# Fused attention and SwiGLU on one core: earlier V loads, AV products behind scores, and FFN partial sums ahead of the last pair

## The chip, the core and the metric

The kernel runs on one core of a Trainium2 chip. A core has five engines that work side by side, each through its own queue in order: TensorE (PE, matrix products into PSUM), VectorE (DVE), ScalarE (ACT), GpSimd (POOL) and SyncE (SP, which here only issues DMAs). DMAs are issued by SP, POOL and ACT, and the data are moved by 16 DMA engines. The metric is the device time of one execution in microseconds (us); lower is better.

## What is computed

Eight batches of eight heads, 576 positions, 64 per head. Per head, a causal attention with a bias from a running sum; then all tokens (4608 of width 512) go through a SwiGLU block with 1536 hidden columns:

```python
scores = scale * np.matmul(q, k.transpose(0, 1, 3, 2))
cum = np.cumsum(np.maximum(s, 0.0), axis=-1)
bias = -(cum[:, :, :, None] - cum[:, :, None, :])
scores = np.where(causal, -1e9, scores + np.minimum(bias, 0.0))
attn = exp(scores - max); attn = attn / (sum + 1e-09)
x = (attn @ v).transpose(0, 2, 1, 3).reshape(B * S, H * D)
g = x @ w_gate
out = (g * sigmoid(g) * (x @ w_val)) @ w_out
```

## The kernel before, in words

**Heads, pairs and blocks.** A head is numbered bh = 8 * batch + head. Four heads make a block hb; a block has two row groups r with two heads e each. Two neighbouring heads make a pair, whose 128 columns are one of the four 128-row slices c of the transposed input XT of the FFN. So a batch has pairs 0 to 3, and the FFN's sums run over c = 0 to 3.

**Keys and queries.** load_one (L148) brings k and q of a block from DRAM on SP's queue into raw tiles, casts (L242, L251) make them bf16, PE transposes them through PSUM (pe_transpose, L285, pe_transpose_half, L296) and pe_out (L309) copies them to KQ. KQ has two buffers, for even and odd blocks. In 64 rows of each KQ tile stand the k and q values of a row group, in the other 64 the bias: zeros, and four rows that aug (L185) copies by DMA from HL, one DMA for each of four heads. HL (L208 to L235) is made on DVE from s: maximum with 0, running sum, and a split into two bf16 parts. The bias so comes out of the same matmul as the score. aug_rows (L181) names the 64 bias rows, pads (L212) zeroes columns behind the sequence, init_vt (L196) sets the ones column and the zero rows of a V tile.

**Scores.** score_piece (L344) makes one of four pieces of a head's transposed scores; in batch 0 two pieces share a bank pair ("wide", 1024 columns of float32), and one exponential on ACT (L380) takes 1024 or 576 columns of it. POOL then zeroes what lies above the diagonal (affine_select, L383 and L388). The result is pt.

**AV.** av_piece (L396 on) multiplies pt by V with a column of ones, in 15 matmuls a head; av_out (L414 on) divides by the sum on DVE into ot. x_pe (L448) transposes a pair's ot on PE and copies it to XT, on ACT or DVE. V of a batch comes by load_v (L163, SP's queue, five chunks of positions) and is cast by cast_v (L174).

**FFN.** ffn_items (L560) handles 512 tokens: for each of 12 slices ft of the hidden columns a gate sum over c = 0 to 3 (L571), tanh on ACT (th, L576), pp on DVE (L578), a value sum (L586) and ht on DVE (L591). Then four blocks of 128 output rows, each a sum of 12 matmuls of 512 columns (L599), scaled on ACT (L616) and stored by POOL (L622). The last block of the last tile is scaled half on DVE and half on ACT and stored by SP and ACT (L610 to L613). The weights come on POOL's queue (w_load, L325), halves j of the hidden columns apart.

**Order.** The program writes the order of every queue by hand. The opening (L195 to L235 and L630 to L650) loads, zeroes and prepares blocks 0 and 1. first_batch (L660) then runs the eight heads of batch 0; after head h come the weight loads of wq and the items of tail: "a" an AV product with its division, "x" the transposition of a pair with an ACT copy, "w" warm-up matmuls on the identity (keep_warm, L652). Before, the AV products stand behind heads 6 and 7. Then second_psum (L131) replaces the PSUM pools (two wide and four single banks) by eight single banks, and the main loop (L725) runs ffn_items with attention of the later batches woven in (attn_items, L522; pump, L710) and with the hooks of L718, which prepare block 2 in the first four steps. take and give (L121, L127) hand out the bank that was given back longest ago.

Of the kernel before, what the change touches and what calls it, by code (L numbers as in the profile page):

```python
# [19 lines left out]
def kernel(  # L20
# [85 lines left out]
    with tc.manual_schedule():  # L106
# [35 lines left out]
        def view(b, w):  # L142
            return bank[b][:, 0:w]
# [59 lines left out]
        load_qk(1)  # L203

# [11 lines left out]
        for r in range(2):  # L216
            nc.gpsimd.memset(aug_rows(0, r)[:, 1, :], 0.0)
            nc.scalar.mul(
                KQ[0][r][64 * (1 - r) : 64 * (1 - r) + 64, 0, :],
                one_s[0:64, 0:1].to_broadcast([64, NR * S + 64]), 0.0,  # L220
            )
        pads(0)
        init_vt(0)
        init_vt(1)
        nc.vector.memset(aug_rows(1, 0), 0.0)
        nc.gpsimd.memset(aug_rows(1, 1), 0.0)
        pads(1)
# [330 lines left out]
        stores = []  # L558

        def ffn_items(tt):  # L560
# [5 lines left out]
            for ft in range(NFT):  # L566
                j, f0 = divmod(ft * 128, WCH)
                gbs = take()
                pg = view(gbs, TT)
                for c in range(4):  # L570
                    nc.tensor.matmul(  # L571
                        pg, WG[j][:, c, f0 : f0 + 128], xt[:, c, :],
                        start=(c == 0), stop=(c == 3),
                    )
# [8 lines left out]
                vbs = take()  # L583
                pv = view(vbs, TT)
                for c in range(4):
# [9 lines left out]
            for ts_ in range(4):  # L595
                ybs = take()
# [10 lines left out]
                a = tt * TT + ts_ * 128  # L607
                if a + 128 == NT:
                    half = DM // 2
                    nc.vector.tensor_scalar_mul(ysb[:, half:DM], py[:, half:DM], 0.5)  # L610
                    nc.scalar.mul(ysb[:, 0:half], py[:, 0:half], 0.5)
                    nc.sync.dma_start(out[a:NT, half:DM], ysb[:, half:DM])
                    nc.scalar.dma_start(out[a:NT, 0:half], ysb[:, 0:half])  # L613
                    give(ybs)
                    return
# [13 lines left out]

        cast_half(0, "k", 0, nc.scalar)  # L630
        cast_half(0, "q", 0, nc.scalar)
        aug(0, SP4)
        load_v(0, range(5))
        load_qk(2)
# [4 lines left out]
        pe_out(0, "k", 1, 0, nc.scalar)  # L639
        pe_out(0, "q", 0, 0, nc.vector)  # L640
        pe_out(0, "q", 1, 0, nc.vector)
        cast_half(0, "k", 1, nc.scalar)
        cast_half(0, "q", 1, nc.gpsimd)
        aug(1, GP4)
        for nm, eng in (("k", nc.scalar), ("q", nc.vector)):
# [5 lines left out]

        def keep_warm(n):  # L652
            bs = take()
            for _ in range(n):
                nc.tensor.matmul(
# [111 lines left out]
```

The softmax here doesn't subtract the row's maximum and nothing guards it: scores larger than these inputs give would overflow.

## Time and profile before

| | us |
|---|---|
| median of 7 runs | 389.39 |
| lowest and highest of them | 388.65, 391.94 |
| the profiled execution | 390.58 |
| its span, first to last instruction | 388.80 |

Of the costliest groups of instructions the page says (time busy, mean of one):

| line, engine | what | number | busy us | mean ns |
|---|---|---|---|---|
| L571 PE | gate matmuls, 512 columns | 424 | 110.4 | 379 |
| L586 PE | value matmuls, 512 columns | 407 | 109.1 | 379 |
| L599 PE | output matmuls, 512 columns | 415 | 103.3 | 379 |
| L380 ACT | exponentials | 224 | 104.2 | 504 |
| L578 DVE | pp | 108 | 74.2 | 687 |
| L591 DVE | ht | 108 | 74.0 | 685 |
| L383 POOL | select, 128x512 | 64 | 41.3 | 645 |
| L190 POOL | issue of kq<-HL | 52 | 31.4 | 604 |

The mean of a matmul is from its start to its modelled end; matmuls overlap, and four of 512 columns follow each other in 0.86 us in the chain of waits. Busy times of one engine add up; those of different engines overlap. The granted TensorE clock is 1.000 over the span. The DMA share is the mean busy share of the 16 DMA engines; in short windows it can stand above 1. A row of the timeline gives start, length, engine, line, operation, output and inputs, number, and in brackets how long the engine was idle before it and what ended that wait. "DMA to landing" is the time from a DMA's issue to its completion.

### The profile page before, as it was taken

What the parts mean: (1) busy time and instruction counts of PE and PEld (TensorE: products, weight loads), DVE (VectorE), ACT (ScalarE), POOL (GpSimd) and SP (SyncE); (2) the same over time, 40 slices, a digit from 0 to 9 for tenths busy, and PEclk for the clock granted to TensorE, in tenths of its full rate; (3) what the DMA queues carried; (4) which work ended last, traced back from release to release, by engine and by line L of the source; (5) the groups of instructions that cost most, each with busy time, mean ns of one, the idle gap of its engine ahead of it and who ended that gap; (6) DMA issues with size and microseconds to landing.
All of it is one profiled execution on the core that took longest, in us unless ns stands there. A gap on an engine that the chain in (4) does not pass through costs nothing.

```text
span 388.8 us, 7878 instructions
## 1 busy us (share of the span) xinstructions
PE 369.4 (95%) x2944; PEld 205.8 (53%) x2994; DVE 240.3 (62%) x431; ACT 214.5 (55%) x411; POOL 192.7 (50%) x329
## 2 busy tenths in 40 slices
PE   3779999999999999999999999999999999999995
PEld 3665556655555555555555555555555544444442
DVE  7766777468653786368735884488347625733750
ACT  8586877567656565566556655665464513323321
POOL 7683368656684856566656666576342220011001
PEclk9999999999999999999999999999999999999999
DMA  7999999995849998895789758965231122002002
GB/s 242 203 241 261 197 282 229 311 265 150 170 143 258 284 234 218 209 276 145 185 212 255 195 152 137 289 156 98 61 113 35 31 73 69 3 27 81 2 12 97
DMA packets 100534, 64.18 MB, mean 165 GB/s; under 512 B 81888, under 2 KB 85824, under 8 KB 100496
## 3 DMA queue, kind: packets, MB, share of 16 engines
q1 hardware_dynamic: 90672, 45.23, 49.2%
q0 software_dynamic: 9680, 18.32, 17.9%
q8 instruction: 23, 0.38, 0.4%
q14 instruction: 15, 0.12, 0.1%
q10 hardware_dynamic: 144, 0.13, 0.1%
HBM read 37.90 MB, written 19.86 MB: 149 GB/s over the span
## 4 chain that ended last, share of the span: by engine, by line
PE 80%; DVE 7%; DMA 5%; issue 4%; ACT 2%; SPq 1%; POOL 0%; DVEq 0%; ACTq 0%; POOLq 0%
PE bank L571 21%; PE bank L586 20%; PE bank L599 20%; PE bank L367 8%; PE bank L405 6%; DMA XT<-xs 2%; DMA pk<-ks 2%; PE wide L367 2%; DVE pp L578 2%; ACT pt L380 1%; DVE ht L591 1%; DVE kq L320 1%; PE one L405 1%; DMA kq<-HL 1%; DMA xs<-ot 1%
## 5 line engine op out<-in xcount | busy, mean ns | idle before, releaser
L380 ACT ACTIVATE pt<-bank 128x512 bf16<-128x512 f32 x224 | 104.2, 504 | 40.3 <-PE bank L367 29.4
L578 DVE SCALAR_TENSOR_TENSOR pp<-th,bank 128x512 bf16<-128x512 bf16 x108 | 74.2, 687 | 69.0 <-ACT th L576 68.2
L571 PE MATMUL bank<-XT,wg 128*128 128x512 bf16 x424 | 110.4, 379 | 1.9 <-DMA XT<-xs 0.9
L586 PE MATMUL bank<-XT,wv 128*128 128x512 bf16 x407 | 109.1, 379 | 1.5 <-DVE pp L578 0.2
L576 ACT ACTIVATE th<-bank 128x512 bf16<-128x512 f32 x108 | 64.5, 597 | 78.3 <-PE bank L571 73.0
L599 PE MATMUL bank<-wo,ht 128*128 128x512 bf16 x415 | 103.3, 379 | 0.9
L591 DVE TENSOR_TENSOR ht<-pp,bank 128x512 bf16<-128x512 bf16 x108 | 74.0, 685 | 8.8
L367 PEld LDWEIGHTS <-kq 128*128 128x128 bf16 x576 | 47.0, 100 | 39.6 <-issue 5.8
L367 PE MATMUL bank<-kq 128*128 128x128 bf16 (+4 forms) x504 | 65.9, 240 | 0.4 <-DVE ht L591 0.2
L383 POOL TENSOR_SCALAR_AFFINE_SELECT pt<-pt 128x512 bf16<-128x512 bf16 x64 | 41.3, 645 | 34.2 <-ACT pt L380 33.6
L571 PEld LDWEIGHTS <-wg 128*128 128x128 bf16 x432 | 38.3, 98 | 36.5 <-issue 1.0
L599 PEld LDWEIGHTS <-ht 128*128 128x128 bf16 x432 | 38.3, 98 | 35.8
L586 PEld LDWEIGHTS <-wv 128*128 128x128 bf16 x432 | 38.4, 98 | 35.1 <-issue 1.1
L405 PEld LDWEIGHTS <-pt 128*128 128x128 bf16 x960 | 41.5, 98 | 21.2 <-issue 0.6
L439 POOL DMA_DIRECT2D xs<-ot x24 | 22.0, 916 | 60.7 <-DVE ot L422 60.7
L622 POOL DMA_DIRECT2D out_dram<-ysb x35 | 19.7, 564 | 60.8 <-ACT ysb L616 60.8
L616 ACT ACTIVATE ysb<-bank 128x512 f32<-128x512 f32 x35 | 20.9, 597 | 40.9 <-PE bank L599 36.5
L405 PE MATMUL bank<-vt,pt 128*128 128x65 bf16 x840 | 42.8, 194 | 0.0
L190 POOL DMA_DIRECT2D kq<-HL x52 | 31.4, 604 | 1.9 <-PE bank L571 1.6
L421 DVE RECIPROCAL rc<-bank 128x5 f32<-128x5 f32 x56 | 10.6, 190 | 34.4 <-PE bank L405 34.4
L422 DVE TENSOR_TENSOR ot<-bank,rc 128x320 bf16<-128x320 f32 x56 | 27.5, 492 | 1.9
L388 POOL TENSOR_SCALAR_AFFINE_SELECT pt<-pt 128x64 bf16<-128x64 bf16 x64 | 16.5, 257 | 21.1 <-ACT pt L380 20.9
(66 smaller groups left out, 207.7 us busy)
## 6 DMA issues: line engine op xcount, KB each, us to landing
out_dram<-ysb POOLq DMA_DIRECT2D x35, 256.0 KB, 3.1
rawk<-in_k_dram SPq DMA_DIRECT2D x15, 576.0 KB
rawq<-in_q_dram SPq DMA_DIRECT2D x15, 576.0 KB
rawv<-in_v_dram SPq DMA_DIRECT2D x32, 256.0 KB
xs<-ot POOLq DMA_DIRECT2D x24, 160.0 KB, 4.0
ks<-ck SPq DMA_DIRECT2D x11, 288.0 KB
qs<-cq SPq DMA_DIRECT2D x11, 288.0 KB
wg<-in_moe_w_gate_dram POOLq DMA_DIRECT2D x2, 768.0 KB, 12.4
```

Of the source, the lines that this page charges most:

```text
L190: engs[hh].dma_start(KQ[hb % 2][r][r0 : r0 + 4, :, e * S : (e + 1) * S], HL[bh : bh + 1, :, :, :],)
L367: nc.tensor.matmul(sc[:, o : o + w], T[:, 1, e * S + 128 * tj : e * S + 128 * (tj + 1)], T[:, 0, e * S + lo : e * S + hi], start=True, sto ...
L380: nc.scalar.activation(pt[:, c0 : c0 + W], sc[:, 0:W], AF.Exp, scale=0.125)
L383: nc.gpsimd.affine_select(pt[:, 1088:1600], pt[:, 1088:1600], pattern=[[0, 4], [1, 128]], compare_op=ALU.is_ge, fill=zreg, base=0, channel ...
L405: nc.tensor.matmul(av[:, bi * (D + 1) : (bi + 1) * (D + 1)], pt[:, c0 : c0 + 128], VT[b % 2][:, tj, h, :], start=(tj == 0), stop=(tj == bi),)
L422: nc.vector.tensor_mul(ot[:, :, e * D : (e + 1) * D], av3[:, :, 0:D], rc[:, :, None].to_broadcast([128, NCH, D]),)
L571: nc.tensor.matmul(pg, WG[j][:, c, f0 : f0 + 128], xt[:, c, :], start=(c == 0), stop=(c == 3),)
L576: nc.scalar.activation(th, pg, AF.Tanh, scale=0.5)
L578: nc.vector.scalar_tensor_tensor(pp, in0=th, scalar=1.0, in1=pg, op0=ALU.add, op1=ALU.mult)
L586: nc.tensor.matmul(pv, WV[j][:, c, f0 : f0 + 128], xt[:, c, :], start=(c == 0), stop=(c == 3),)
L591: nc.vector.tensor_mul(ht, pp, pv)
L599: nc.tensor.matmul(py, hts[ft][:, ts_ * 128 : (ts_ + 1) * 128], WO[ft // WKO][:, ft % WKO, :], start=(ft == 0), stop=(ft == NFT - 1),)
```

## The change

- The loads of V of batch 0 and of q,k of block 2 stand right behind those of block 1 on SP's queue.
- The four bias DMAs of block 0 are issued by ACT (one) and POOL (three) instead of SP, behind ACT's copies of k.
- Zeroing: for block 0 one half is moved from ACT to DVE; that of block 1, its pads and the second V tile's constants go to POOL, behind the preparation of block 0.
- V's five casts go to DVE (chunks 0 to 2) and POOL (3 and 4), and stand earlier in the program.
- Ten warm-up matmuls come ahead of block 0's first scores; the two groups ahead of the FFN are gone.
- AV products of heads 0 to 3 stand behind the scores of heads 3 to 6; pair 0's copy to XT is on DVE.
- second_psum stands ahead of AV product 4. ffn_pre(c) makes the matmuls of slice c of the first two gate and value sums of the first tile, for c = 0 to 2, before or just behind pair 3's transposition; ffn_items takes up these sums at c = 3.
- The first half of the gate and value weights is loaded in two parts, behind heads 1 and 3.
- The last 128 output rows are made in two banks of 256 columns, the first scaled on ACT, the second on DVE, both stored by SP.

```diff
         load_qk(1)
+        load_v(0, range(5))
+        load_qk(2)
...
-        for r in range(2):
-            nc.gpsimd.memset(aug_rows(0, r)[:, 1, :], 0.0)
-            nc.scalar.mul(
-                KQ[0][r][64 * (1 - r) : 64 * (1 - r) + 64, 0, :],
-                one_s[0:64, 0:1].to_broadcast([64, NR * S + 64]), 0.0,
-            )
+        nc.gpsimd.memset(aug_rows(0, 0)[:, 1, :], 0.0)
+        nc.scalar.mul(
+            KQ[0][0][64:128, 0, :],
+            one_s[0:64, 0:1].to_broadcast([64, NR * S + 64]), 0.0,
+        )
         pads(0)
+        nc.gpsimd.memset(aug_rows(0, 1)[:, 1, :], 0.0)
+        nc.vector.memset(aug_rows(0, 1)[:, 0, :], 0.0)
         init_vt(0)
-        init_vt(1)
-        nc.vector.memset(aug_rows(1, 0), 0.0)
-        nc.gpsimd.memset(aug_rows(1, 1), 0.0)
-        pads(1)
...
+        def ffn_pre(c):
+            for ft in range(2):
+                for kind, W in enumerate((WG, WV)):
+                    bs = take() if c == 0 else pre[0, ft, kind][0]
+                    pre[0, ft, kind] = (bs, c + 1)
+                    nc.tensor.matmul(
+                        view(bs, TT), W[0][:, c, ft * 128 : ft * 128 + 128], XT[:, c, 0:TT],
+                        start=(c == 0), stop=False,
+                    )
...
-                gbs = take()
+                gbs, c0 = pre.pop((tt, ft, 0)) if (tt, ft, 0) in pre else (take(), 0)
                 pg = view(gbs, TT)
-                for c in range(4):
+                for c in range(c0, 4):
...
+                a = tt * TT + ts_ * 128
+                if a + 128 == NT:
+                    half = DM // 2
+                    for i in range(2):
+                        ybs = take()
+                        py = view(ybs, half)
+                        cols = slice(i * half, (i + 1) * half)
+                        for ft in range(NFT):
+                            nc.tensor.matmul(
+                                py, hts[ft][:, ts_ * 128 : (ts_ + 1) * 128],
+                                WO[ft // WKO][:, ft % WKO, cols],
+                                start=(ft == 0), stop=(ft == NFT - 1),
+                            )
+                        ysb = yp.tile([128, half], FP32, tag="yh", bufs=2, name="yh")
+                        if i == 0:
+                            nc.scalar.mul(ysb, py, 0.5)
+                        else:
+                            nc.vector.tensor_scalar_mul(ysb, py, 0.5)
+                        nc.sync.dma_start(out[a:NT, cols], ysb)
+                        give(ybs)
+                    return
...
         cast_half(0, "k", 0, nc.scalar)
         cast_half(0, "q", 0, nc.scalar)
-        aug(0, SP4)
-        load_v(0, range(5))
-        load_qk(2)
         for nm in ("k", "q"):
             for g in range(2):
                 pe_transpose_half(0, nm, g, 0)
         pe_out(0, "k", 0, 0, nc.scalar)
         pe_out(0, "k", 1, 0, nc.scalar)
+        aug(0, [nc.scalar] + [nc.gpsimd] * 3)
+        keep_warm(10, "w")
...
         cast_half(0, "k", 1, nc.scalar)
         cast_half(0, "q", 1, nc.gpsimd)
+        nc.gpsimd.memset(aug_rows(1, 0), 0.0)
+        nc.gpsimd.memset(aug_rows(1, 1), 0.0)
+        pads(1)
         aug(1, GP4)
+        init_vt(1)
...
+        cast_v(0, 0, nc.vector)
+        cast_v(0, 1, nc.vector)
...
-            wq = {1: (("g", 0), ("v", 0)), 4: (("g", 1),), 5: (("v", 1),)}
+            wq = {
+                1: (("g", 0, 0), ("v", 0, 0)), 3: (("g", 0, 1), ("v", 0, 1)),
+                4: (("g", 1),), 5: (("v", 1),),
+            }
             tail = {
-                6: ("a0", "a1"),
-                7: ("a2", "a3", "a4", "x0", "a5", "x1", "a6", "a7", "x2", "w6", "x3", "w8"),
+                3: ("a0",), 4: ("a1",), 5: ("a2",), 6: ("a3", "d0"),
+                7: (
+                    "p0", "a4", "x1", "a5", "a6", "a7", "x2", "f0", "x3", "f1", "f2",
+                ),
             }
...
+                if h == 1:
+                    cast_v(0, 3, nc.gpsimd)
+                    cast_v(0, 4, nc.gpsimd)
...
                     for r in range(2):
                         for nm, g in order:
                             pe_out(1, nm, g, r, nc.vector)
-                    for c in range(3, 5):
-                        cast_v(0, c, nc.vector)
-                if h == 2:
-                    for c in range(3):
-                        cast_v(0, c, nc.gpsimd)
+                        if r == 0:
+                            cast_v(0, 2, nc.vector)
```

In the new tail, "p0" stands for second_psum(), "d0" for x_pe(0) with its copy on DVE, and "f" with a number c for ffn_pre(c).

## The prediction

> **What bounds the kernel now.** I read the share of busy time first, then busy time and clock in stretches of 10 us, then the chain of waits and the timeline of the stretches in which TensorE (PE) isn't full.
>
> From the page, and from the windows of 10 us (sum, then busy us and instructions of PE, weight loads, DVE, ACT, POOL; clock, DMA share, GB/s):
> ```profile
> PE 369.4 (95%) x2944; PEld 205.8 (53%) x2994; DVE 240.3 (62%) x431; ACT 214.5 (55%) x411; POOL 192.7 (50%) x329
> 0.00:10.00 10.00, 3.99 (x35) 3.61 (x36) 7.72 (x13) 8.09 (x11) 7.32 (x20) 1.00 0.75 242
> 10.00:20.00 10.00, 7.55 (x58) 5.78 (x57) 7.51 (x11) 5.74 (x8) 6.26 (x13) 1.00 0.95 213
> 20.00:30.00 10.00, 8.18 (x169) 7.04 (x169) 6.26 (x18) 8.32 (x12) 8.99 (x16) 1.00 1.15 230
> 40.00:50.00 10.00, 9.25 (x70) 5.31 (x70) 7.55 (x11) 8.83 (x18) 3.18 (x6) 1.00 1.21 199
> 380.00:390.00 10.00, 4.57 (x22) 1.86 (x19) 0.42 (x1) 1.01 (x3) 1.08 (x2) 0.99 0.22 79
> ```
> PE is full from 50 to 380 us, at clock 1.00; the change leaves that work alone. It can only win or lose in the first 50 us and behind the last matmul. There the timeline shows what PE waits for:
> ```profile
> 7.94 2.92 SPq L190 DMA_DIRECT2D kq<-HL  x4
> 22.01 0.95 PE L367 MATMUL wide<-kq 128*128 128x128 bf16 x9 [0.77 <-ACT pt L380]
> 31.02 0.53 PE L455 MATMUL one<-ident,ot 128*128 128x128 bf16 x5 [0.18 <-DVE ot L422]
> 34.02 0.69 DVE L578 SCALAR_TENSOR_TENSOR pp<-th,bank 128x512 bf16<-128x512 bf16 x1 [3.05 <-ACT th L576]
> 41.38 0.68 DVE L578 SCALAR_TENSOR_TENSOR pp<-th,bank 128x512 bf16<-128x512 bf16 x1
> 42.11 1.02 PE L571 MATMUL bank<-XT,wg 128*128 128x512 bf16 x4 [0.21 <-DVE pp L578]
> ```
> The bias rows (kq<-HL) are issued at 7.94, when HL is done, and the first score starts at 11.06. From 17.5 to 27.6 us ACT's exponentials set the pace, 1.71 a head, and PE idles 0.77 in each. Then the AV products, x0 to x3 and warm-up matmuls run until the first FFN matmul at 32.28. From 34.02 to 42.85 DVE has no gap: pp, ht and the kq copies of the next pairs. At 42.11 PE waits for DVE. That stretch decides what a lead of PE is worth.
>
> **Start.** *HL.* DVE zeroed 64x1216 (1.07 us, 2.50 to 3.57) ahead of the s_sb operation at 3.60; now half of it, by the row 0.54. The operation comes between 3.07 (s already there) and 3.60 (s landed only then); the trace shows no wait that would tell. HL is done between 7.31 and 7.84; I take 7.6. *Bias rows.* SP's four issues become one on ACT (about 0.37, the row of ACT's last output DMA) and three on POOL (0.604 each, 1.8 in all). Both engines must wait for HL, and queue work behind that wait: ACT its cast of k half 1 (7.40 before, 8.0 now), POOL its cast of q half 1 (8.48 before, when q landed; now 7.65+1.8 = 9.45). The q transposes, ahead of the first score in PE's order, go from 9.20 to about 10.15, and last 1.17: the score comes at about 11.25 instead of 11.06, **+0.2**. The ten new warm-up matmuls (0.085 each by the old ones, 0.51 for six) end before the k transposes can start.
>
> The landing is the unknown. In the trace of before, head 0's rows landed 3.08 after issue. On POOL's queue I asked at three times: 9.15, 55.8 and 91.5 us.
> ```profile
> DMA to landing us min/median/max: 2.1/2.6/3.6
> DMA to landing us min/median/max: 5.4/6.7/7.5
> DMA to landing us min/median/max: 2.0/2.4/3.5
> ```
> The DMA share around them was 0.8 falling to 0.2, 1.0, and 0.6. **A rule against the change**: the Trainium skill, "DMA: Bandwidth & Descriptors", section "Issuing engines are not separate DMA queues", says that transfers from any engine interleave on the same 16 DMA engines, so leaving SP's queue saves only issue time. By the rule the rows share those engines with q,k 1 and with V, which now follows without the gap of 10 to 12 us (share 0.37 and 0.19): the busy row's 5.4 to 7.5. By the rows, head 0 (ACT) lands at 7.65+3.08 = 10.7, hidden behind the q transposes; head 1 (POOL, first issue) is wanted at 13.4 and lands at 7.65+5.4 = 13.05, just in time. I take 3.08 for head 0, the nearest row (same transfer, same microseconds, share 1.0), and 5.4 for head 1. Ends: 2.0 gains nothing, as the transposes hide it; 7.5 costs 1.8 (head 1) to 4 (head 0). Heads 2 and 3 have till 16.6.
>
> **A second rule against it**: "SBUF — State Buffer", section "Summary: rules for kernel authors", wants a transfer that is to hide under DVE work issued from ACT or SP, since GpSimd's descriptor writing starves while DVE is in a fast mode. If each of three issues stood behind a whole DVE copy (0.72), the start would lose 3x0.72 = 2.2. The row: POOL's issues at 9.15 to 11.7 ran beside DVE's kq copies at 9.98 to 11.44 and took 0.586 to 0.752; at worst 0.15 each. The row decides, +0.0 to +0.4.
>
> *Moved past SP.* V's five loads (0.89 each on SP) and q,k 2 no longer wait for HL; q,k 1 is drained at about 10.5, a V chunk of 256 KB flows at 205 to 283 GB/s in 1.0 to 1.25 us, so V is in by about 16 and 17.5 with a completion like that of q half 1 (bytes by 7.0, wait ended 8.48). DVE takes casts of chunks 0 and 1 behind its casts of q,k 1 (ends near 15.2; it had idled 2.43 before its copy at 15.34) and chunk 2 between the copies of r=0 and r=1 (done 22.0, head 6 wants it at 23.9). No cost; with that cover gone a late chunk delays head 4's copies one for one.
>
> *POOL's queue.* From 9.45: cast 0.67, two zeroings 1.10, pads 0.44, aug(1) 4x0.604, init_vt(1) 0.8, two selects 0.78, V chunks 3 and 4 1.1: about 18.7. a0 is wanted at 19.7. Then six weight issues of 0.77 (four before; I give half loads the price of whole ones) and selects: head 6 at 27.2, head 7 at 28.0, as before. POOL's idle time is used up; each further delay lands on a6 or a7.
>
> **AV behind the scores.** a0 to a3 cost PE 0.56 each (x15) in gaps of 0.77; a3 with d0 is 0.91, where 1.08 (two AVs at 24.51) already fitted. They leave the tail. Behind head 7's scores (26.4+0.2) PE has a4 to a7 (4x0.56), x1 to x3 (3x0.35), f0 to f2 (12x0.216) and the first c=3 matmul, 0.22: 6.1 us, gapless if POOL is on time, so first gate ready at 32.7 against 33.3. The old warm-ups (0.51 and 0.62) lay in waits. Then th (0.6) and pp: pp0 at 33.4 instead of 34.02, **-0.6**. With POOL late by 0.9, or WV's first half (issued 19.5 instead of 16.9, landing 13.7 before for twice the bytes) later than f0 at 29.5, it is 0. I take **-0.5**.
>
> **Partial sums.** They bring PE to the third gate 2.4 us earlier (36.73 to 34.3: 2.0 of work done ahead, 0.4 of the shift). But DVE needs 8x0.69 for pp and ht and 3.1 for kq copies whatever PE does. Eight banks are taken in turn, the gate at 42.11 takes the bank that pp at 41.38 frees, and that order stays. PE waits there longer, and only pp0's 0.5 goes through. What is late next is DVE.
>
> **End.** The last 512 columns become two groups of 256: 24 matmuls of 108 ns against 12 of 216, +0.05. Before:
> ```profile
> 384.67 0.42 DVE L610 TENSOR_SCALAR ysb<-bank 128x256 f32<-128x256 f32 x1 [9.18 <-PE bank L599]
> 385.12 0.33 SPq L612 DMA_DIRECT2D out_dram<-ysb  x1
> 385.13 0.38 ACT L611 ACTIVATE ysb<-bank 128x256 f32<-128x256 f32 x1 [2.51 <-DVE ysb L610]
> 385.54 0.37 ACTq L613 DMA_DIRECT2D out_dram<-ysb  x1
> ```
> ACT's half followed DVE's by 0.43 and its DMA ended the run. Now ACT's half is done under the second group and SP issues last at 385.17: **-0.4**.
>
> **Sum**: the start's +0.2 is inside pp0's -0.5; with -0.4 it is -0.9. The profiled execution, 390.58 (span 388.80 and 1.78 around it), becomes 389.7. The median of the runs is 1.19 lower, 389.39, and becomes **388.5**.
>
> **Rivals.**
> - *PE's lead survives* (28 in 100): DVE catches up, or PE finds a free bank at 41 us. For it: DVE idles 1.36 at 42.85. Against: that idle comes after PE's wait, and DVE has none before it. Then -2.4-0.4 = -2.8: 386.6.
> - *Bias rows late* (20 in 100): the rule on shared queues wins. It decides from a landing of head 0 after 11.95, 4.3 us from issue (0.9 is then eaten). At 6.7, the busy median, it is 14.35, +3.1-0.9: 391.8; at 5.4, 390.5; head 1 alone at 7.5, 390.3.
> - *The AVs don't fit*: a0 waits for V chunk 4 on POOL. Each us behind 19.9 goes into ACT's pace; POOL would have to lose 1.2. It lies in the ranges.
> - *The edit does nothing at the front*: pp0 at 34.0, only the end pays: 389.0. Part of the forecast.
>
> **How the numbers follow.** Forecast 52 in 100, with its own range 387.6 to 389.6 (pp0 from -0.9 to +0.4, end -0.3 to -0.5). A measurement of this kernel tells about 0.5% from no change, 1.95 us. Faster by more (below 387.44): the lead's 28, a little of it short, and the forecast's low edge: 0.31. Slower by more (above 391.34): late rows beyond 6.2 us: 0.13. Same: 0.56. Range 386.4 to 391.0: it leaves out the later half of the late rows and a thin edge below.
>
> **What would show it.** The first score near 11.25 (later than 12: the rows); no ACT gap behind 17.7; pp0 at 33.4, DVE gapless behind it, and a PE wait of about 2 us near 39 to 41.5 for ht or pp. If PE doesn't wait there, I am wrong on the lead; if POOL's select of head 7 comes after 29, on POOL. At the end, the last DMA 0.4 sooner behind the last matmul.

## The result and the profile after

| | before | after |
|---|---|---|
| median of the runs, us | 389.59 (31 runs, 388.21 to 391.94) | 392.90 (12 runs, 392.08 to 394.57) |
| the profiled execution, us | 390.58 | 392.88 |
| its span, us | 388.8 | 391.1 |

The kernel became slower: ratio 1.0088, 95% interval 1.007 to 1.0106, or 3.3 us. The forecast was 388.5 and its range ended at 391.0. The two profiled executions differ by 2.3 us, since the profiled one of before was itself 1.0 above its median; those two traces can account for 2.3 of the 3.3. The trace of e4 (below), whose program is that of before up to the last 128 rows and whose profiled execution took 389.70, close to the median of before, accounts for 3.2.

From the page of the kernel after, the busy time of each engine:

```profile
PE 367.9 (94%) x2952; PEld 206.0 (53%) x3002; DVE 241.2 (62%) x433; ACT 212.8 (54%) x409; POOL 197.3 (50%) x334
```

TensorE does nearly the same work (eight matmuls more: four warm-ups fewer, twelve more for the last rows). From the windows of the kernel after (the columns are those of the prediction's windows):

```profile
0.00:10.00 10.00, 3.92 (x35) 3.24 (x36) 6.64 (x12) 5.96 (x8) 4.83 (x15) 1.00 0.78 243
10.00:20.00 10.00, 6.44 (x60) 5.17 (x58) 5.68 (x9) 4.53 (x7) 9.62 (x17) 0.66 1.10 252
20.00:30.00 10.00, 6.99 (x113) 5.60 (x111) 7.27 (x16) 9.20 (x12) 9.95 (x20) 1.00 0.94 133
40.00:50.00 10.00, 7.58 (x56) 4.32 (x56) 7.79 (x13) 7.97 (x16) 3.53 (x7) 1.00 1.20 201
```

Three things to see. PE is busy 1.1 us less in 10 to 20 us, and its clock has a mean of 0.66 there. POOL has no idle time left from 10 to 30 us (9.62 and 9.95 of 10, before 6.26 and 8.99). And in 40 to 50 us PE idles 2.4 us where it idled 0.75.

**The start**, from the timeline of the kernel after:

```profile
4.48 9.10 SPq L169 DMA_DIRECT2D rawv<-in_v_dram  x5
...
7.61 1.22 ACTq L190 DMA_DIRECT2D kq<-HL  x1
8.22 1.95 POOL L190 DMA_DIRECT2D kq<-HL  x3 [4.23 <-DVE kq L319]
8.87 0.67 ACT L256 CAST ck<-rawk 128x576 bf16<-128x576 f32 x1 [1.28 <-DVE kq L319]
...
13.91 1.51 PE L366 MATMUL wide<-kq 128*128 128x128 bf16 x9 [2.28 <-DMA kq<-HL]
```

The first score starts at 13.9 instead of 11.06, and PE stood ready 2.28 us before it, waiting for the bias rows. They were issued at 7.61, so head 0's row took about 6.3 us, where that of before took 3.1. POOL's copies of the rows were slow as well; for kq in the first 32 us the kernel after has this, where before has 2.1/2.6/3.6:

```profile
DMA to landing us min/median/max: 5.3/5.7/6.2
```

**The tail of batch 0 and the first FFN sums**, from the timeline of the kernel after:

```profile
25.15 4.99 ACT L379 ACTIVATE pt<-wide 128x1024 bf16<-128x1024 f32 x6
...
30.19 0.61 PE L404 MATMUL bank<-vt,pt 128*128 128x65 bf16 x15 [1.31 <-ACT pt L379]
...
34.43 0.64 ACT L459 COPY XT<-bank 128x576 bf16<-128x576 bf16 x1 [0.69 <-PE bank L454]
...
36.06 0.38 PE L581 MATMUL bank<-XT,wg 128*128 128x512 bf16 x1
...
37.11 0.69 DVE L588 SCALAR_TENSOR_TENSOR pp<-th,bank 128x512 bf16<-128x512 bf16 x1 [3.37 <-ACT th L586]
...
42.34 0.82 PE L366 MATMUL bank<-kq 128*128 128x128 bf16 x8 [1.87 <-DVE kq L319]
...
44.48 0.68 DVE L588 SCALAR_TENSOR_TENSOR pp<-th,bank 128x512 bf16<-128x512 bf16 x1
```

PE goes from 30.19 to the first gate sum with one gap of 0.16, but it starts 1.31 us late: the AV product of head 4 is the first to use the new PSUM pools, and it waits until the last exponential of batch 0 has ended (30.14). The first pp stands at 37.11 instead of 34.02. From there DVE needs the same time as before to its fourth pp (37.11 to 45.16, 8.05 us; before 34.02 to 42.06, 8.04), and PE, which is ahead, waits 1.87 us for DVE's kq copy.

**The end**, from the timeline of the kernel after:

```profile
383.99 2.78 PE L614 MATMUL bank<-wo,ht 128*128 128x256 bf16 x24
...
385.50 0.39 ACT L621 ACTIVATE yh<-bank 128x256 f32<-128x256 f32 x1 [0.71 <-PE bank L614]
385.91 1.69 SPq L624 DMA_DIRECT2D out_dram<-yh  x2
386.81 0.42 DVE L623 TENSOR_SCALAR yh<-bank 128x256 f32<-128x256 f32 x1 [9.14 <-PE bank L614]
```

From the end of the last matmul to the end of the span it takes 4.37 us; before it took 4.26. Nothing was gained there.

### The profile page after: what moved, and what is told of

Same layout as the page of the kernel before. It is cut to its first block, busy times and chain, and to the rows that moved or that the text cites. A ratio compares the mean times of both kernels' runs of the same rounds, so it can differ in the third digit from the quotient of the medians.

```text
span 391.1 us, 7896 instructions
## 1 busy us (share of the span) xinstructions
PE 367.9 (94%) x2952; PEld 206.0 (53%) x3002; DVE 241.2 (62%) x433; ACT 212.8 (54%) x409; POOL 197.3 (50%) x334
## 4 chain that ended last, share of the span: by engine, by line
PE 81%; DVE 4%; issue 3%; DMA 2%; POOL 0%; ACT 0%; DVEq 0%; POOLq 0%; ACTq 0%; SPq 0%
PE bank L581 22%; PE bank L596 21%; PE bank L630 20%; PE bank L366 9%; PE bank L404 7%; DVE pp L588 1%; DVE ht L601 1%; DVE kq L319 1%; DMA XT<-xs 1%; DMA xs<-ot 1%; PE bank L565 1%; PE bank L614 1%; PE bank L454 1%; PE bank L290 0%; DVE kq L277 0%
## 5 line engine op out<-in xcount | busy, mean ns | idle before, releaser
L581 PE MATMUL bank<-XT,wg 128*128 128x512 bf16 x403 | 108.2, 379 | 2.3 <-DMA XT<-xs 0.7
L630 PE MATMUL bank<-wo,ht 128*128 128x512 bf16 x404 | 99.5, 379 | 0.8
L630 PEld LDWEIGHTS <-ht 128*128 128x128 bf16 x420 | 37.1, 98 | 34.4
L404 PE MATMUL bank<-vt,pt 128*128 128x65 bf16 x900 | 44.9, 194 | 1.4 <-ACT pt L379 1.3
L190 POOL DMA_DIRECT2D kq<-HL x55 | 33.3, 607 | 4.5 <-DVE kq L319 4.2
L420 DVE RECIPROCAL rc<-bank 128x5 f32<-128x5 f32 x60 | 11.4, 190 | 36.7 <-PE bank L404 36.5
L421 DVE TENSOR_TENSOR ot<-bank,rc 128x320 bf16<-128x320 f32 x60 | 29.5, 492 | 2.1
```

The costliest lines, as they stand in the source:

```text
L190: engs[hh].dma_start(KQ[hb % 2][r][r0 : r0 + 4, :, e * S : (e + 1) * S], HL[bh : bh + 1, :, :, :],)
L404: nc.tensor.matmul(av[:, bi * (D + 1) : (bi + 1) * (D + 1)], pt[:, c0 : c0 + 128], VT[b % 2][:, tj, h, :], start=(tj == 0), stop=(tj == bi),)
L421: nc.vector.tensor_mul(ot[:, :, e * D : (e + 1) * D], av3[:, :, 0:D], rc[:, :, None].to_broadcast([128, NCH, D]),)
L581: nc.tensor.matmul(pg, WG[j][:, c, f0 : f0 + 128], xt[:, c, :], start=(c == 0), stop=(c == 3),)
L630: nc.tensor.matmul(py, hts[ft][:, ts_ * 128 : (ts_ + 1) * 128], WO[ft // WKO][:, ft % WKO, :], start=(ft == 0), stop=(ft == NFT - 1),)
```

## The experiments

The theory, from the two traces: the change loses at the start, where V's loads now stand ahead of the bias rows, and the sums ahead of pair 3 bring nothing. Rivals: the new queues (ACT, POOL) are slow, not V; the pool change is the loss, not the start; POOL's longer queue is. Each ratio below is to the kernel before, with its 95% interval. Line numbers in the rows are those of each experiment's own program.

### e1 and e2: the rows first, on the old queue and on the new ones

Both put V and the loads of block 2 behind the rows again. e1 leaves the rows on SP as before, e2 on ACT, POOL (two) and SP (the last).

```diff
         load_qk(1)
-        load_v(0, range(5))
-        load_qk(2)
...
-        aug(0, [nc.scalar] + [nc.gpsimd] * 3)
+        aug(0, SP4)                                            # e1
+        aug(0, [nc.scalar, nc.gpsimd, nc.gpsimd, nc.sync])     # e2
+        load_v(0, range(5))
+        load_qk(2)
```

> The changed kernel with the start's order of before: all four bias DMAs of block 0 on SP, V and q,k 2 behind them; casts, AV order, partial sums and end stay as changed. Theory 1 (the late bias rows are the loss): the first score comes at 10.6 to 11.2 us instead of 13.90, the exponentials of batch 0 end about 2.5 us sooner, and the time falls by 2.5 to 3.5 us, to 0.991 to 1.001 of before. Theory 2 (the new order behind the scores is the loss: PE waits 1.31 us for the last exponential, because the PSUM pools change ahead of AV product 4): the first score may come sooner, but most of the loss stays, ratio 1.005 to 1.009. Also told here: whether the transpositions of block 1 run in 1.0 us instead of 1.9 when PE has not cooled before them.

> The changed kernel with head 0's bias row on ACT, heads 1 and 2 on POOL as changed, head 3 on SP, and V and q,k 2 behind that SP DMA, so that nothing of V is in flight when the rows are issued. If the loads ahead of the rows make them late: landing 2 to 3.6 us from issue, first score at 10.6 to 11.4, ratio as in the run with all rows on SP. If the queues that issue them (ACT, POOL) are what is slow: ACT's issue takes 1.22 us again, landing 5 to 6 us, first score after 13, ratio 1.006 to 1.010.

e1: 391.62, ratio 1.0055 (1.0031 to 1.0078). e2: 392.31, 1.007 (1.0046 to 1.0094). From the timeline of e1, and then of e2:

```profile
7.54 2.89 SPq L190 DMA_DIRECT2D kq<-HL  x4
...
11.63 1.51 PE L364 MATMUL wide<-kq 128*128 128x128 bf16 x9 [1.59 <-DMA kq<-HL]
```

```profile
7.61 1.45 ACTq L190 DMA_DIRECT2D kq<-HL  x1
...
8.40 5.01 SPq L169 DMA_DIRECT2D rawv<-in_v_dram  x5
...
11.64 0.86 PE L364 MATMUL wide<-kq 128*128 128x128 bf16 x9 [0.62 <-DMA kq<-HL]
...
18.77 0.43 PE L402 MATMUL one<-vt,pt 128*128 128x65 bf16 x9 [0.94 <-DVE kq L317]
19.95 0.76 PE L402 MATMUL one<-vt,pt 128*128 128x65 bf16 x6 [0.75 <-POOL vt L176]
...
22.22 1.57 ACT L377 ACTIVATE pt<-wide 128x1024 bf16<-128x1024 f32 x2 [3.14 <-PE wide L364]
```

The first score is at 11.63 in one and 11.64 in the other, against 13.9. That they agree so closely is chance: e11 (below) has e1's opening and its first score at 10.88. But over all runs the two orders don't overlap. With V ahead of the rows the first score is at 13.26 to 14.28 (the change, e3, e5, e9), with the rows ahead at 10.50 to 11.66 (before and all the others). So the order costs some 2.3 us, and the choice of queue at most 0.8. Of the loads that moved it is V's that count: in the change those of block 2 are issued only from 13.62 on. The total gains only 1.3 (e1) and 0.6 (e2) of the 3.3, and by the times alone even that isn't sure, as the intervals overlap that of the change. In e1 the scores of heads 0 to 2 ran at half the TensorE clock, so that head 2's exponential came at 18.08 (before 17.50), and the tail behind the exponentials is as slow as the change's. e2 shows another loss. Its start is not only early but at full clock (nine score matmuls in 0.86 us), and then the AV product of head 0 stands in PE's queue ahead of head 4's scores and waits, 0.94 us for a kq copy of DVE and 0.75 for V's cast on POOL; ACT idles 3.14 us behind it.

### e3: the PSUM pools changed two products later

```diff
-                    "p0", "a4", "x1", "a5", "a6", "a7", "x2", "f0", "x3", "f1", "f2",
+                    "a4", "x1", "a5", "p0", "a6", "a7", "x2", "f0", "x3", "f1", "f2",
```

> The changed kernel with the change of PSUM pools behind AV product 5 instead of ahead of AV product 4, so that a4, x1 and a5 don't take banks of the new pools. Theory 1 expects the first score still at 13.9; a4 to a5 fill the idle 1.31 us ahead of 30.19, the first pp comes 0.9 to 1.3 us sooner than 37.11, and the whole gains that: ratio about 0.997 against the changed kernel, 1.005 to 1.007 against before. Theory 2 expects the same sign but most of the loss gone: ratio below 1.003. If the wait has another source than the pools, nothing moves (1.007 to 1.010).

393.24, 1.0085 (1.0058 to 1.0112): as slow as the change within the interval. The first pp comes at 36.66, 0.45 sooner than in the change and not the 0.9 to 1.3 expected. From the timeline of e3:

```profile
31.18 1.07 PE L404 MATMUL bank<-vt,pt 128*128 128x65 bf16 x30 [0.90 <-DVE ot L421]
```

The wait moved from the product of head 4 (1.31, for ACT's last exponential) to that of head 6 (0.90, for the division of head 5's product). The reading that fits both is that the first tile of a new pool waits for the last use of the old ones, which in both places is work just issued. In before the pools change behind pair 3's transposition, and there the first gate waits only 0.17, for ACT's copy.

### e4: the end alone, on the kernel before

```diff
-                    nc.vector.tensor_scalar_mul(ysb[:, half:DM], py[:, half:DM], 0.5)
-                    nc.scalar.mul(ysb[:, 0:half], py[:, 0:half], 0.5)
-                    nc.sync.dma_start(out[a:NT, half:DM], ysb[:, half:DM])
-                    nc.scalar.dma_start(out[a:NT, 0:half], ysb[:, 0:half])
...
+                    for i in range(2):
...
+                        nc.sync.dma_start(out[a:NT, cols], ysb)
```

> The kernel before with nothing but the last output in two banks, both stored by SP. The prediction's term: 0.4 us sooner (ratio 0.999), the end of the span 3.8 us behind the last matmul instead of 4.2. The rival, from the two traces (before: SP issue at 385.12 to the end 3.68; changed: SP's last issue at 387.27 to the end 3.83): SP's store, not ACT's, ended the run before, so nothing is gained: ratio 1.000, end 4.2 to 4.4 us behind the last matmul.

389.59, 1.0004 (0.999 to 1.0017). This interval still holds the 0.4 us of the forecast, but the trace doesn't: from the last matmul to the end of the span it takes 4.23 us, in before 4.26. From the timeline of e4, whose span ends at 387.99:

```profile
382.89 1.69 SPq L614 DMA_DIRECT2D out_dram<-yh  x2
383.79 0.42 DVE L613 TENSOR_SCALAR yh<-bank 128x256 f32<-128x256 f32 x1 [9.14 <-PE bank L604]
```

ACT's half is indeed done under the second group of matmuls, and SP's last store is issued at 384.25, 0.5 us behind the last matmul (383.75), where the last issue of before came 0.96 behind it. Yet from SP's last issue to the end of the span it takes 3.74 us here (3.88 in the change). In before, SP's store was issued at 385.12, 3.7 us ahead of the end, and ACT's at 385.54, only 3.3 us ahead of it. The reading that fits all three is that SP's store ended the run of before too, and ACT's, issued later, had landed sooner. The trace has no completion for these two, so this is argued; that the edit brings nothing behind the last matmul is seen.

e4 also serves as a second execution of before's front. Rows of ht (the DVE operation that ends a hidden slice) at the same two places of each program, first of before:

```profile
92.79 0.69 DVE L591 TENSOR_TENSOR ht<-pp,bank 128x512 bf16<-128x512 bf16 x1
128.88 0.69 DVE L591 TENSOR_TENSOR ht<-pp,bank 128x512 bf16<-128x512 bf16 x1
```

Then of e4, with its first pp:

```profile
33.86 0.69 DVE L578 SCALAR_TENSOR_TENSOR pp<-th,bank 128x512 bf16<-128x512 bf16 x1 [3.05 <-ACT th L576]
...
92.62 0.69 DVE L591 TENSOR_TENSOR ht<-pp,bank 128x512 bf16<-128x512 bf16 x1
127.89 0.69 DVE L591 TENSOR_TENSOR ht<-pp,bank 128x512 bf16<-128x512 bf16 x1
```

And of the change:

```profile
95.59 0.69 DVE L601 TENSOR_TENSOR ht<-pp,bank 128x512 bf16<-128x512 bf16 x1
130.86 0.69 DVE L601 TENSOR_TENSOR ht<-pp,bank 128x512 bf16<-128x512 bf16 x1
```

With the same program there, e4 gains 0.8 us on before between 93 and 128 us: one execution differs from another by that much. Against e4 the change is 3.25 late at the first pp, 2.97 at both places and 3.15 at the end of the span.

### e5: the change without the partial sums

```diff
-                    "p0", "a4", "x1", "a5", "a6", "a7", "x2", "f0", "x3", "f1", "f2",
+                    "p0", "a4", "x1", "a5", "a6", "a7", "x2", "x3",
```

> The changed kernel without the partial sums (f0, f1, f2); the FFN's sums start at c = 0 as before. If DVE bounds the stretch behind the first pp, the work done ahead is worth nothing, and the eight matmuls of f1 and f2 only stand between pair 3's copy and the first whole gate: the first pp comes 1.0 to 1.8 us sooner than 37.11, behind a first score at 13.9, PE's wait for DVE near 43 shrinks from 2.4 us to below 0.8, and the ratio against before falls from 1.0088 to 1.004 to 1.006. If PE's lead is worth something, the ratio stays or rises (1.009 to 1.012).

392.11, 1.0069 (1.0045 to 1.0093), more than the 1.004 to 1.006 expected, and the interval overlaps the change's; it is the trace that shows the cost. From the timeline of e5:

```profile
22.21 6.70 ACT L379 ACTIVATE pt<-wide 128x1024 bf16<-128x1024 f32 x8 [0.34 <-PE wide L366]
...
34.87 0.69 DVE L588 SCALAR_TENSOR_TENSOR pp<-th,bank 128x512 bf16<-128x512 bf16 x1 [2.36 <-ACT th L586]
```

Batch 0's exponentials end at 28.91 and the first pp is at 34.87, 5.96 us later; with the sums it is 30.14 and 37.11, 6.97. The sums cost 1.0 us there: two of the three groups stand ahead of the first gate, which could have started when ACT had copied pair 3 (34.43 + 0.64 = 35.07) and started at 36.06. And what they bring behind it is lost: DVE needs 8.05 us from its first to its fourth pp in both, and without the sums PE waits for no kq copy (0.16 for ht and 0.21 for pp are its only waits from 36 to 46 us).

### e9, e10, e12, e7: one part alone, on the kernel before

e9 is the start: V and the block-2 loads ahead of the rows, the rows on ACT and POOL, nothing else.

```diff
         load_qk(1)
+        load_v(0, range(5))
+        load_qk(2)
...
-        aug(0, SP4)
-        load_v(0, range(5))
-        load_qk(2)
...
+        aug(0, [nc.scalar] + [nc.gpsimd] * 3)
```

> The kernel before with only the start's loads changed: V of batch 0 and q,k 2 right behind q,k 1, and the bias rows of block 0 on ACT (one) and POOL (three). If the loads in front of the bias rows are the main loss: first score at 13.3 to 14.0 us, first pp 2.2 to 2.9 us later than in the kernel before on the same chip, ratio 1.005 to 1.008. If the loss needs the other parts (POOL's queue, AV order, pools), below 1.003.

392.01, 1.0063 (1.0045 to 1.0081). From the timeline of e9:

```profile
7.99 1.24 ACTq L190 DMA_DIRECT2D kq<-HL  x1
...
14.28 1.51 PE L369 MATMUL wide<-kq 128*128 128x128 bf16 x9 [1.81 <-DMA kq<-HL]
```

Here too the row lands 6.3 us after its issue and PE waits for it. The rest of the stretch is as before, only later: the exponentials of heads 2 to 7 run without a gap and the first pp is at 36.41. The start alone makes most of the loss.

e10 is the partial sums with the early pool change.

```diff
-                7: ("a2", "a3", "a4", "x0", "a5", "x1", "a6", "a7", "x2", "w6", "x3", "w8"),
+                7: ("a2", "a3", "p0", "a4", "x0", "a5", "x1", "a6", "a7", "x2", "f0", "x3", "f1", "f2"),
...
+                        ffn_pre(i)
```

> The kernel before with only the partial sums: the PSUM pools change ahead of AV product 4, f0 before and f1, f2 behind pair 3's transposition, no warm-up there. If the pool change holds PE and DVE absorbs the lead: PE idle about 1.3 us ahead of AV 4 until head 7's exponential ends, first pp 0.5 to 1.5 us later, a wait of PE for DVE of about 2 us near 40, ratio 1.001 to 1.004. If the sums help: first pp sooner or PE without that wait, 0.994 to 0.998.

390.95, 1.0047 (1.003 to 1.0064). From the timeline of e10:

```profile
26.39 0.61 PE L405 MATMUL bank<-vt,pt 128*128 128x65 bf16 x15 [1.07 <-DVE ot L422]
...
30.89 0.38 PE L567 MATMUL bank<-XT,wg 128*128 128x512 bf16 x1 [0.91 <-DMA wv<-in_moe_w_val_dram]
...
39.79 0.82 PE L367 MATMUL bank<-kq 128*128 128x128 bf16 x8 [1.66 <-DVE kq L320]
```

Two costs are in it, the pools' wait of 1.07 and a wait for the weights of 0.91, and PE's lead brings nothing, for it ends in a wait for DVE of 1.66. The first pp comes only 0.5 later than in before because the scores of this execution ran faster (see the table below); from the last exponential on it takes 2.5 us longer.

e12 is the work moved to POOL: zeroings, pads and V constants of block 1, and the weights' first half in two parts.

```diff
-        init_vt(1)
-        nc.vector.memset(aug_rows(1, 0), 0.0)
-        nc.gpsimd.memset(aug_rows(1, 1), 0.0)
-        pads(1)
...
+        nc.gpsimd.memset(aug_rows(1, 0), 0.0)
+        nc.gpsimd.memset(aug_rows(1, 1), 0.0)
+        pads(1)
         aug(1, GP4)
+        init_vt(1)
...
-            wq = {1: (("g", 0), ("v", 0)), 4: (("g", 1),), 5: (("v", 1),)}
...
+                1: (("g", 0, 0), ("v", 0, 0)), 3: (("g", 0, 1), ("v", 0, 1)),
```

> The kernel before with only POOL's queue changed: both zeroings of block 1, its pads and the second V tile's constants behind the cast of q half 1, ahead of and behind the rows of block 1, and the first weights loaded in halves behind heads 1 and 3. If POOL's queue costs by itself: selects and AV products late at the end of batch 0, first pp 0.3 to 1.5 us later, ratio 1.001 to 1.004. If its idle time takes it up: 0.999 to 1.001.

389.93, 1.002 (1.0006 to 1.0034). From the timeline of e12:

```profile
26.25 0.63 PE L401 MATMUL one<-vt,pt 128*128 128x65 bf16 x15 [0.56 <-POOL pt L379]
...
27.79 1.40 PE L401 MATMUL one<-vt,pt 128*128 128x65 bf16 x30 [0.55 <-POOL pt L379]
```

POOL's queue is so late that its selects hold two AV products for 1.1 us. In the kernel before PE waits for no select from 15 to 36 us, and in e10, whose exponentials end about as early as e12's (25.67 and 25.21), it waits for none either.

e7 is the AV products behind scores, one head later than in the change, with V's casts on DVE (two) and POOL (three) to serve them.

```diff
-                6: ("a0", "a1"),
-                7: ("a2", "a3", "a4", "x0", "a5", "x1", "a6", "a7", "x2", "w6", "x3", "w8"),
+                4: ("a0",), 5: ("a1",), 6: ("a2", "a3"),
+                7: ("a4", "d0", "x1", "a5", "a6", "a7", "x2", "w6", "x3", "w8"),
```

> The kernel before with only the AV products moved: heads 0 and 1 behind the scores of heads 4 and 5, heads 2 and 3 behind head 6's, pair 0's copy on DVE, V's casts a little earlier (two on DVE, three on POOL); loads, bias rows, pools and FFN as before. The prediction's step: the tail loses two AV products, so the gate is ready 0.5 to 1.1 us sooner, ratio 0.997 to 0.999. The rival, that the tail is a chain from head 7's exponential through AV 7, DVE, pair 3's transposition and ACT, 4.6 us whatever PE does before it: 0.999 to 1.001.

388.76, 0.9993 (0.9977 to 1.0009), which can't be told from before and can't decide between the two. The trace speaks for the prediction's step: from the last exponential of batch 0 to the first pp it takes 5.64 us, in before 6.38. It is the best of all kernels tried, and no part of the change that could be tried alone does better.

### e11: the change with the old start, and neither sums nor early pool change

```diff
-        load_v(0, range(5))
-        load_qk(2)
...
-        aug(0, [nc.scalar] + [nc.gpsimd] * 3)
+        aug(0, SP4)
+        load_v(0, range(5))
+        load_qk(2)
...
-                    "p0", "a4", "x1", "a5", "a6", "a7", "x2", "f0", "x3", "f1", "f2",
+                    "a4", "x1", "a5", "a6", "a7", "x2", "x3", "p0",
```

> The changed kernel with bias rows on SP and V and q,k 2 behind them, without the partial sums, and with the pools changed behind pair 3 as before. What is left of the change: zeroing and casts on POOL and DVE, the split weight loads, AV products behind heads 3 to 6, ten warm-ups, two banks at the end. If the start and the sums explain the loss: 0.998 to 1.002. If POOL's longer queue (weights issued 3 to 5 us later, the rows of block 1 at 13 instead of 9 us) costs by itself: 1.003 to 1.006.

390.51, 1.0028 (1.0016 to 1.0041), between the two forecasts. From the timeline of e11:

```profile
15.36 0.43 DVE L176 CAST vt<-rawv 128x512 bf16<-128x512 f32 x1 [1.07 <-DMA rawv<-in_v_dram]
...
18.96 2.82 DVE L317 COPY kq<-one 64x640 bf16<-64x640 bf16 x4
19.44 0.61 POOL L176 CAST vt<-rawv 64x512 bf16<-64x512 f32 x1 [0.79 <-DMA rawv<-in_v_dram]
19.84 0.98 PE L402 MATMUL one<-vt,pt 128*128 128x65 bf16 x15 [2.77 <-DVE kq L317]
...
21.71 1.56 ACT L377 ACTIVATE pt<-wide 128x1024 bf16<-128x1024 f32 x2 [3.39 <-PE wide L364]
```

With the rows first, V comes later. Its casts on DVE wait for it (0.89 at 13.85, 1.07 at 15.36) and stand ahead of the kq copies, one of which frees the PSUM tile that head 0's product needs; POOL casts the last chunk only at 19.44. The product stands in PE's queue ahead of head 4's scores, and ACT idles 3.39 us. So the placement of the products behind head 3 needs V early, and V early makes the rows late. This holds where the first heads run at full clock, as here and in e2: e1, with e11's opening and half the clock until 18.3, has no such gap. e7, which puts the first product one head later, has a gap of only 0.47 us there.

### e6 and e8: the clock of the first scores, on the kernel before

Since the first scores of before ran slower than the later ones (1.51 us for nine against 0.95, see below), e6 adds warm-up matmuls: ten behind block 0's first transposes and sixteen behind its second. e8 is e6 and e7 together.

```diff
         pe_out(0, "k", 1, 0, nc.scalar)
+        keep_warm(10, "w")
...
                 pe_out(0, nm, g, 1, eng)
+        keep_warm(16, "w")
```

> The kernel before with nothing but warm-up matmuls on the identity: ten behind the first transpositions of block 0, sixteen behind the second, so that PE doesn't idle until the bias rows land. If the clock is what makes the first heads slow (the run with V held had 4.2 us from the first score to head 2's exponential, the others 6.4): first score at 11.1 to 11.6, the 18 transpositions of block 1 in 1.0 us instead of 1.9, head 2's exponential at 15.3 to 15.9 instead of 17.50, first pp 1.5 to 2.2 us sooner, ratio 0.994 to 0.997. If something else sets the pace there, 0.999 to 1.001.

> Both of the last two edits on the kernel before. If they add up: first pp 2.0 to 3.3 us sooner than 34.02, ratio 0.991 to 0.996. If POOL's queue or the bias rows of block 1 take over once the first heads are faster (as in the run with V held, where head 4's scores waited for rows and AV 0 for a V cast), the gain of the warm-up alone is not exceeded, and PE waits for kq<-HL or for a V cast at 18 to 21 us.

e6: 390.79, 1.0032 (1.0014 to 1.005). e8: 390.98, 1.0035 (1.002 to 1.005). From the timeline of e6:

```profile
11.44 0.85 PE L367 MATMUL wide<-kq 128*128 128x128 bf16 x9
...
124.93 0.38 PE L571 MATMUL bank<-XT,wg 128*128 128x512 bf16 x1 [1.95 <-DMA XT<-xs]
```

The scores run at full rate (0.85 for nine, 1.51 before), and the first pp comes at 32.10, 1.9 us ahead of before. But the lead doesn't last: the DVE operation that ends a hidden slice is 1.9 us ahead of its place in before up to 54 us, 1.2 ahead at 83, 0.1 behind at 127 and 1.5 behind from 147 us on. At 124.93 PE waits 1.95 us for the DMA that transposes x; in before, that wait is 0.35. With the AV products added (e8) the first pp is at 32.15 and the total is that of e6.

### The front in one table

Times from the profiled executions, us from the start of each span:

| | first score | exponential of head 2 | first pp | tail | ratio |
|---|---|---|---|---|---|
| before | 11.06 | 17.50 | 34.02 | 6.38 | 1 |
| the change | 13.90 | 19.95 | 37.11 | 6.97 | 1.0088 |
| e9 start alone | 14.28 | 19.90 | 36.41 | 6.38 | 1.0063 |
| e10 sums alone | 10.96 | 15.54 | 34.55 | 8.89 | 1.0047 |
| e12 POOL's moves alone | 10.50 | 15.08 | 33.07 | 7.85 | 1.002 |
| e7 AV alone | 11.09 | 15.67 | 31.77 | 5.64 | 0.9993 |
| e4 end alone | 11.29 | 17.34 | 33.86 | 6.38 | 1.0004 |
| e5 change without sums | 13.26 | 18.59 | 34.87 | 5.96 | 1.0069 |
| e11 rest of the change | 10.88 | 15.04 | 33.83 | 5.18 | 1.0028 |

The tail is the time from the end of batch 0's last exponential to the first pp. It leaves out the speed of the first scores, which differs from execution to execution; e4, e6 and e9, whose programs are that of before in this stretch, all have 6.38, and e1 and e2, whose tail is that of the change, have 6.97. So the change loses 2.85 us at the first score, most of which e9 loses alone, takes 0.35 less than before from there to the last exponential, and loses 0.59 in the tail: 3.09 at the first pp. In the tail the AV products behind scores bring 1.20 (e11), the early pool change takes 0.78 (e5 against e11, which differ in the opening too) and the partial sums 1.01 (the change against e5).

The single parts add up to 0.0127 (0.0063 + 0.0047 + 0.002 - 0.0007 + 0.0004), the whole is 0.0088. Part of this is seen: where the start is 2.8 us late, POOL and V have the time that e12, e2 and e11 lack: the tails of e10 and e12 are 2.5 and 1.5 us longer than that of before, where the change's is 0.6 longer. The change also has no gap of ACT over 0.2 us from 19.95 to the end of batch 0. The front's times also depend on the clock in the one execution that was profiled (17.50 against 15.1 to 15.7 in the second column, with the first score within 0.6), so a row of this table isn't a measurement of its ratio.

## Why the prediction was wrong

**What failed: the landing of head 0's row.** The step was: "I take 3.08 for head 0, the nearest row (same transfer, same microseconds, share 1.0), and 5.4 for head 1." It measured 6.3 from the issue, 5.1 even from the end of it. The row was the nearest by transfer and time, but not by what was in flight: in before V started at 10.90, behind the rows, and the change put five V loads ahead of them. Nor was its share 1.0 for long. While that row was on its way in before, the DMA share in the windows of 1 us from 9 to 12 was 0.83, 0.37 and 0.19; in the change it is 1.03, 1.20 and 1.27. The rule that the prediction weighed against it, that transfers of all issuing engines share the same DMA engines (the Trainium skill, "DMA: Bandwidth & Descriptors", section "Issuing engines are not separate DMA queues"), agrees with the runs: changing the queue made at most 0.8 us, changing the order some 2.3. By it the busy rows of the trace, 5.4 to 7.5, would have held: a landing of 6.3 behind the prediction's 7.65 is 13.95, and the score came at 13.91. That was the rival "Bias rows late", given 20 in 100. (Its sum is 0.2 too high: 389.39 + 3.1 - 0.9 is 391.6, and the landing of 5.4 gives 390.3.)

**The rest of the start.** HL at 7.6: it was done at 7.44. One issue on ACT at 0.37: it took 1.22 (1.24 in e9, 1.45 in e2), so ACT's cast of k came at 8.87 instead of 8.0. POOL's three issues at 0.604: 0.65 each, but from 8.22; the 2.2 us that waiting behind DVE's copies would have cost didn't come (DVE was copying beside the first of the three only). PE stood ready 2.28 before the row was there, so these delays cost nothing more; the first score was forecast for 11.25 (the forecast's own steps, 10.15 + 1.17, give 11.32) and came at 13.90.

**AV behind the scores.** That the products fit the gaps was right: ACT's only gap behind 19.95 is 0.20, though with a start 2.8 us late this was an easier test than the one forecast. That PE's tail is 6.1 us long was right too: 30.19 to 36.28. "Gapless" was wrong at its first step, and this is the second step that failed: the pool change was moved ahead of head 4's product, and the prediction gave it no cost. The wait is 1.31 (0.90 in e3, 1.07 in e10), and 0.78 of it reaches the first pp by e5 against e11. With the late start (+2.65 on the forecast) and the wait of 1.31, the first pp forecast for 33.5 would come at 37.5; it came at 37.11.

**Partial sums.** That DVE's work takes up PE's lead was right, and the rival that the lead survives fell: 8.05 us from first to fourth pp with or without it, and PE waits 1.87 for kq. The prediction had the 2.6 us of the sums in its tail, but it never set that tail against one without them. e5 does: the sums cost 1.0 us ahead of the first gate and bring nothing behind it.

**POOL's queue.** "Used up" was right, and "each further delay lands on a6 or a7" nearly so: in e12, with the rest as before, the selects held two products for 0.56 and 0.55. In the change itself, with its late start, PE waits for no select.

**V's casts.** "No cost; with that cover gone a late chunk delays head 4's copies one for one": the first half was seen in the change, with its late start, and a late chunk in e11, where ACT idles 3.39. Whether that is one for one no run tells.

**End.** Forecast -0.4; nothing was gained behind the last matmul (e4). The step "its DMA ended the run", that is ACT's, most likely took the wrong DMA for the last.

**The sum.** Forecast -0.5 at the first pp and -0.4 at the end. Against the trace of before the change is 3.09 late at the first pp, 2.80 from 54 to 93 us, 1.99 from 127 us on and 2.3 at the end. The fall by 0.8 is not the change's doing, for e4 gains as much on before in the same stretch. Against e4 the change is 3.25 late at the first pp and 3.15 at the end. So the prediction's frame, that PE is full from 50 us on and the front passes through unchanged, held for this loss, and the 3.2 us between the two executions are close to the 3.3 of the medians. It did not hold for the leads of e6 and e7 (see the last section).

## What to carry to other kernels

A short transfer on the critical path is priced by what will be in flight when it is issued: where a change puts bulk loads ahead of it, the nearest row is one taken among bulk loads, not the same transfer in the old order, and another queue didn't help here. Work pulled forward on an engine that waits for a slower one further on gained nothing here, and it costs what it delays of that engine's first input. Of a bundle of edits each wants a test alone: here the parts that looked free cost 0.5% (the sums with their pool change) and 0.2% (a fuller POOL queue) or brought nothing (the last store).

## What was not expected of the hardware

**The clock of the first scores.** The page's clock row says 1.00 for the start of before, but nine score matmuls took 1.51 us at 11.06 and 0.95 at 18.58, so the clock column isn't to be trusted that early. In the change the clock had come up behind the warm-up matmuls (nine transposes take 0.69 at 9.60, 1.17 at 5.19), and it was lost again. From the windows of 1 us of the change:

```profile
11.00:12.00 1.00, 0.62 (x9) 0.46 (x9) 0.56 (x1) 0.45 (x1) 1.00 (x1) 1.00 1.27 235
12.00:13.00 1.00, 0.00 (x0) 0.00 (x0) 0.97 (x3) 0.00 (x0) 0.95 (x2) 0.77 1.25 222
13.00:14.00 1.00, 0.09 (x2) 0.10 (x3) 1.00 (x2) 0.00 (x0) 0.96 (x3) 0.50 1.25 186
```

PE idles from 11.63, the clock falls to 0.50 between 12 and 13 us and stays there until 19.4. From the first score to head 2's exponential it took 6.05 us so (6.44 in before); with a clock at full from the start it took 4.2 (e2, e6). So the warm-ups bought nothing in this execution. That the wait for the rows lost the clock isn't shown: in e1, whose rows came 2.3 us sooner, nine scores took 1.51 at 11.63 too, with a clock of 0.50. And the moment at which the clock changes isn't that of the program alone. e11 has e1's opening, and its nine scores took 0.86 at 10.88. e3 has the change's opening, and its transposes still took 1.17 at 9.61. e7 opens as before does, and nine scores took 0.95 at 13.24 there, in before still 1.51 at 16.41.

**A front gain isn't always passed on.** In e6 a lead of 1.9 us at 32 us became a lag of 1.5 at 147 us, with a wait of PE of 1.95 on a transposing DMA; in e7 a lead of 2.25 at the first pp became 1.3, with such a wait of 1.07 at 123.51. Part of this is the execution and not the program, as e4 shows by gaining 0.8 on before there. What holds the transposing DMAs up wasn't tried.

**DMA issue times.** The issue of a store on ACT took 0.37 us at the end of before, that of a row 1.22 to 1.45 at 7.6 to 8.0 us, while SP and POOL issue too. SP's five issues of V took 9.1 us where they took 4.45 in before.
